# Score matmuls of a gated-linear-attention kernel moved from two single PSUM banks to one tile of two banks, with a new order of all steps

## The chip, the cores and the metric

One core of a Trainium2 chip runs the whole program. The metric is the device time of one execution in microseconds (us). The engines named below are TensorE (PE; its weight loads appear as PEld), VectorE (DVE), ScalarE (ACT), GpSimd (POOL), and SyncE (SP), which here issues all DMA transfers. PSUM, the memory that PE writes into, has eight banks of 512 fp32 values in each of 128 partitions.

## What is computed

The first part is a recurrent gated linear attention over 4 batches, 8 heads, 768 tokens and head size 48. Its output, laid out as 3072 tokens by 384, goes through a feed-forward block of width 2048 with a hard-swish between its two matrices. All values are fp32.

```python
def _attn_ref(q, k, v, alpha):
    B, H, S, D = q.shape                       # 4, 8, 768, 48
    state = np.zeros((B, H, D, D), dtype=np.float32)
    y = np.zeros_like(q)
    for t in range(S):
        state = alpha[:, :, t, :, None] * state + np.einsum('bhd,bhe->bhde', k[:, :, t], v[:, :, t])
        y[:, :, t] = np.einsum('bhd,bhde->bhe', q[:, :, t], state)
    return y

def _moe_ref(x, w_in, w_out):                  # x: 3072 x 384
    h = x @ w_in                               # 384 x 2048
    g = h * np.clip(h + 3.0, 0.0, 6.0) / 6.0
    return g @ w_out                           # 2048 x 384
```

## The kernel before, in words

**Tiles.** The tokens are cut into 24 chunks of 128 (6 for each batch), and the eight heads into four pairs, so that a tile has two heads in its partitions and four pairs along its free dimension. Two chunks make a group for the feed-forward block; there are 12 groups.

**The recurrence of one chunk j.** The names are those of the steps in the order at the end of the program.

- `la`, `lk`, `lq`, `lv` load alpha, k, q and v on SP. For the first six chunks `ta`, `tk` and `tq` transpose alpha, k and q on PE into a PSUM bank (L282); from chunk 6 on VectorE transposes them (L286), and PSUM isn't used for it.
- `ca` copies alpha out of PSUM (ScalarE, L300). `r` and `p` are scans over alpha on VectorE (L309 with the reciprocal at L313, and L320): products of the decays from the right and from the left. `k` and `q` multiply k and q with them (L332).
- `sc` computes the scores k times q on PE (L346), 64 by 64 tokens at a time: for each pair p, each half chunk b and each head a of the pair. `m` multiplies them with the triangular mask on VectorE (L356) and puts them into the tile `A`. `qa` copies q next to them (ScalarE, L366).
- `kb` and `ck` bring k by token: for chunks 0 to 7 by a transpose on PE (L374) and a copy on ScalarE (L378), from chunk 8 on through memory outside the core (`kt` on VectorE at L391, the writes `kw` at L396 and the reads `kr` at L404, both on SP).
- `u` computes the state's updates on PE (L429), `sm` adds them (VectorE, L437 and L439), `st` applies the decay (POOL, L409), and `sv` copies the state next to v (ScalarE, L419).
- `ya` and `yb` compute the outputs of the two half chunks on PE (L455), and `cy` copies them to `xT` (ScalarE, L464).

**The feed-forward block.** Groups 0 and 1 use plain products for the first matrix (`f`, `fa`, `fb`; L478 and L489), and group 0 also for the second (`b`, L516). All other products are fast matrix products that trade multiplications for sums: `M` (L600) with sums of the first weights (`y`), of x (`xc`), copies (`n`) and sums of the products (`o`); `P` (L703) with sums of the second weights (`x`) and of the hidden values (`s`), copies (`K`) and output sums (`G`). `O` stores outputs on SP. `e` and `h` are the hard-swish on ScalarE and VectorE (`fr` and `fg` in the plain part). `w` loads one of 16 slices of the weights, which come as float64; `d1`, `d2`, `dx` (ScalarE), `d3` (VectorE) and `d4` (POOL) turn a slice into fp32.

**PSUM.** Four banks `m0` to `m3` belong to the feed-forward block. The other four, `t0` to `t3` (L223), hold one thing at a time each: transposes, scores (two banks, one for each head of a pair), updates (one or two banks) or outputs. The numbers at the end of a step name them: `sc.0.2.3` puts the scores of chunk 0 into `t2` and `t3`, `u.0.2.1` its updates into `t2` and `t1`, `ya.0.3` its outputs into `t3`. A bank can be written again when the engine that reads it has ended.

**The order.** The program is one long list of some 1,800 such steps (from L751 on), and each engine runs its own steps in the order of the list. An instruction that waits holds up everything behind it on its engine. `z.m.n` are n matmuls of the identity with itself into bank m, which compute nothing (L532); the trace has two PE instructions for each of them.

The parts of the list that the change and the prediction's steps touch are its head up to the second feed-forward step, and its last lines:

```python
run("""z.0.5 z.0.3 z.0.1 z.0.8 qa.0.0 w.0 d2.0 d3.0 la.0 ta.0.0 ca.0 r.0 lk.0 tk.0.1 k.0
       z.0.2 p.0 la.1 ta.1.2 lq.0 tq.0.3 ca.1 r.1 lk.1 lv.0.0 sv.0.0 d1.0 kb.0.0 ck.0 z.0.2
       u.0.2.1 sm.0.0 sv.0.1 q.0 qa.0.1 tk.1.0 k.1 p.1 z.0.2 sc.0.2.3 m.0 la.2 ta.2.0 ca.2
       dx.0 w.2 d2.2 kb.1.0 ck.1 lq.1 r.2 sm.0.1 st.1 tq.1.2 q.1 d3.2 z.0.3 d1.2 dx.2 lv.1.1
       u.1.3.1 sv.1.0 sm.1.0 p.2 sm.1.1 sc.1.0.2 m.1 ya.0.3 yb.0 cy.0 lq.2 w.1 d1.1 tq.2.1
...
       P.11.4 G.11.1.2 P.11.5 G.11.2.1 O.11.2 P.11.6 G.11.3.0 O.11.3 O.9.2 O.11.1""")
```

Of the kernel before, what the change touches and what calls it, by code (L numbers as in the profile page):

```python
# [8 lines left out]
FP = mybir.dt.float32  # L9
# [4 lines left out]
ALU = mybir.AluOpType  # L14
# [3 lines left out]
def kernel(  # L18
# [32 lines left out]
    nc = tc.nc  # L51
    B, H, S, D = q.shape
    NTOK, DM = out.shape
    C = 128
    NC = S // C
    NCH = B * NC
    NP = H // 2
# [3 lines left out]
    G = 2  # L61
    GT = G * C
    HB = C // 2
# [12 lines left out]
    mask = consts.tile([C, C], mybir.dt.bfloat16, tag="mask")  # L76
# [146 lines left out]
    banks = [ps.tile([C, NP * C], FP, tag=f"t{i}", name=f"t{i}_ps") for i in range(4)]  # L223
# [5 lines left out]
    def bank(name, j, i):  # L229
        ps_t[name, j] = banks[i].rearrange("r (p n) -> r p n", p=NP)  # L230
        return ps_t[name, j]
# [106 lines left out]
    def scores(j, *at):  # L338
        sc = ps_t["sc", j] = [banks[i][:, 0 : NP * HB].rearrange("s (p t) -> s p t", p=NP)
                              for i in at]  # L340
        for p in range(NP):
            for b in range(2):
                half = slice(HB * b, HB * b + HB)
                for a in range(2):
                    r = slice(64 * a, 64 * a + D)
                    nc.tensor.matmul(sc[a][half, p], K_t[j][r, p, half], Q_t[j][r, p, half],  # L346
                                     start=True, stop=True)

    def masked(j):
        A_t[j] = As[j % 2]  # L350
        sc = ps_t.pop(("sc", j))
        for b in range(2):
            half = slice(HB * b, HB * b + HB)
            to = A_t[j][half, b].rearrange("s (p a) t -> s a p t", a=2)
            for a in range(2):
                nc.vector.tensor_tensor(  # L356
                    out=to[:, a], in0=sc[a][half],
                    in1=mask[half, half].unsqueeze(1).to_broadcast([HB, NP, HB]), op=ALU.mult)
# [386 lines left out]
    def run(words):  # L745
        for word in words.split():
            name, *at = word.split(".")
            steps[name](*(int(x) for x in at))

    with tc.manual_schedule():  # L750
        run("""z.0.5 z.0.3 z.0.1 z.0.8 qa.0.0 w.0 d2.0 d3.0 la.0 ta.0.0 ca.0 r.0 lk.0 tk.0.1 k.0  # L751
               z.0.2 p.0 la.1 ta.1.2 lq.0 tq.0.3 ca.1 r.1 lk.1 lv.0.0 sv.0.0 d1.0 kb.0.0 ck.0 z.0.2
               u.0.2.1 sm.0.0 sv.0.1 q.0 qa.0.1 tk.1.0 k.1 p.1 z.0.2 sc.0.2.3 m.0 la.2 ta.2.0 ca.2
               dx.0 w.2 d2.2 kb.1.0 ck.1 lq.1 r.2 sm.0.1 st.1 tq.1.2 q.1 d3.2 z.0.3 d1.2 dx.2 lv.1.1
               u.1.3.1 sv.1.0 sm.1.0 p.2 sm.1.1 sc.1.0.2 m.1 ya.0.3 yb.0 cy.0 lq.2 w.1 d1.1 tq.2.1
               q.2 d4.2 lk.2 tk.2.3 k.2 fa.2.0 d4.0 st.2 sc.2.0.2 d2.1 d3.1 m.2 dx.1 d4.1 qa.1.1
               lk.3 la.3 ta.3.1 ca.3 la.4 fa.0.1 sv.1.1 w.3 r.3 ta.4.3 ca.4 r.4 tk.3.1 k.3 kb.2.0
               qa.1.0 d2.3 ya.1.2 yb.1 cy.1 fa.1.2 lq.3 ck.2 d1.3 p.3 d3.3 lv.2.2 u.2.3.2 sm.2.0
               d4.3 fb.2 tq.3.1 q.3 fb.1 qa.2.0 sm.2.1 sv.2.0 st.3 fr.0.2.0 fg.0.2 lk.4 tk.4.0
               sv.2.1 w.5 d2.5 k.4 d3.5 d1.5 qa.3.0 d4.5 qa.2.1 sc.3.1.3 m.3 w.6 d2.6 d1.6 d3.6 d4.6  # L760
               lv.3.0 lq.4 w.7 kb.3.2 fb.0 f.0.3.3 kb.4.0 ya.2.1 ck.3 u.3.3.2 sm.3.0 fr.0.3.1 fg.0.3
               fr.0.1.0 fg.0.1 qa.3.1 sv.3.0 sm.3.1 p.4 d2.7 sv.3.1 d1.7 d3.7 d4.7 f.0.5.0 fr.0.5.1
               fr.0.0.0 fg.0.5 fg.0.0 tq.4.3 ck.4 la.5 ta.5.2 f.0.6.3 ca.5 w.4 d2.4 ya.3.0 yb.3 cy.3
               fr.0.6.1 yb.2 cy.2 w.9 d2.9 q.4 qa.4.1 d1.4 d1.9 dx.4 la.6 w.8 d3.4 r.5 lk.5 w.10
               d3.9 p.5 ca.6 fg.0.6 d4.9 w.12 lq.5 lv.4.1 d2.8 d3.8 f.0.7.2 d1.8 st.4 d4.8 d4.4 w.11
               fr.0.7.0 fg.0.7 f.1.7.0 fr.1.7.1 fg.1.7 sc.4.0.2 m.4 f.1.1.1 fr.1.1.0 fg.1.1 f.1.3.3
               fr.1.3.1 d2.10 d1.10 tk.5.3 f.1.0.2 d2.12 d3.10 d4.10 w.13 fg.1.3 fr.1.0.0 fg.1.0 k.5
               d3.12 lq.6 f.1.6.0 f.1.2.1 u.4.1.0 sm.4.0 d1.12 d4.12 sv.4.0 qa.4.0 ya.4.2 fr.1.6.1
               fg.1.6 w.15 tq.5.3 fa.4.3 sv.4.1 d2.11 kb.5.1 d2.13 fr.1.2.0 f.1.4.2 fr.1.4.1 d1.11
               sm.4.1 q.5 r.6 d3.11 d3.13 fg.1.4 d4.11 lv.5.0 lk.6 tq.6 p.6 d2.15 d3.15 fg.1.2 d1.13  # L770
               d4.13 sc.5.0.3 yb.4 f.1.5.0 fr.1.5.1 fg.1.5 tk.6 m.5 b.1.0.2 fb.4 b.1.1 d1.15 d4.15
               st.5 y.5 w.14 la.7 lk.7 cy.4 d2.14 qa.5.1 ck.5 b.0.0.1 fr.0.4.0 d3.14 k.6 q.6 ca.7
               fg.0.4 d1.14 d4.14 x.0 y.1 y.10 b.0.1 y.0 y.2 u.5.2 P.1.0.0 K.1.0 qa.5.0 sv.5.0
               qa.6.1 P.1.1.3 b.0.2 b.1.2 kb.6.0 ya.5.3 y.6 s.1.0.0 sm.5.0 sv.5.1 G.1.0.0 tk.7
               s.1.1.1 s.1.2.3 x.1 yb.5 cy.5 b.1.3 sc.6.1.2 lv.6.2 ck.6 u.6.3.0 s.1.3.2 x.2 P.1.2
               b.0.3 K.1.1 y.7 s.1.4 s.1.5 y.11 y.3 r.7 xc.2.1 x.3 y.4 y.8 xc.2.3 k.7 xc.2.0 xc.2.4
               y.9 y.12 y.16 y.13 y.15 P.1.3.3 K.1.2 P.1.4 bo.1 P.1.5 xc.2.5 G.1.1.1 P.1.6 y.14 y.17
               y.19 xc.2.6 sm.6.0 G.1.2.2 y.20 M.2.0.2 lv.12.1 la.8 O.1.1 O.1.0 ca.8 y.18 y.21 y.23
               so.1 G.1.3.3 n.2.0.8 bo.0 lq.7 lv.7.0 O.1.2 m.6 xc.2.2 xc.2.10 xc.2.7 tq.7 r.8 p.7
               xc.2.8 sv.6.1 M.2.15.3 M.2.1 kb.7.3 n.2.1.9 M.2.16 M.2.2 n.2.2.10 M.2.7.0 n.2.7.11  # L780
               sm.6.1 xc.2.9 q.7 p.8 M.2.3 M.2.4 n.2.4.12 M.2.8 o.2.0.0 M.2.5 n.2.5.13 qa.7.0 sv.6.0
               st.7 lk.8 O.1.3 lq.8 lk.9 la.9 la.10 tk.8 tq.8 lq.10 lq.9 ya.6.1 yb.6 M.2.9 z.1.3
               M.2.18.1 o.2.1.0 e.2.1.1 M.2.10 cy.6 ck.7 sc.7.0.2 u.7.1.3 n.2.10.14 M.2.11 qa.7.1
               ca.9 la.11 y.22 M.2.6.2 h.2.1 q.8 m.7 e.2.0.0 h.2.0 n.2.11.15 qa.6.0 n.2.18.10 qa.8.1
               M.2.12 M.2.19 n.2.12.12 M.2.13 sm.7.0 sv.7.1 r.9 k.8 o.2.3.0 sv.7.0 ya.7.0 y.24
               o.2.5.0 n.2.13.12 o.2.2.0 yb.7 cy.7 sc.8.1.2 xc.3.1 o.2.2.1 e.2.2.1 xc.3.3 o.2.3.1
               M.2.14 xc.3.4 xc.3.0 xc.3.5 o.2.4.0 xc.3.7 xc.3.6 o.2.6.0 P.2.0.1 M.3.0.2 M.2.17
               h.2.2 o.2.6.1 e.2.3.0 h.2.3 o.2.7.0 K.2.0 n.3.0.12 M.3.1 n.3.1.9 e.2.5.1 M.3.7.0
               n.3.7.13 xc.3.8 o.2.7.1 xc.3.2 kt.8 e.2.6.0 h.2.6 tk.9 M.3.2 n.3.2.10 e.2.4.0 P.2.1.3
               h.2.4 h.2.5 s.2.0.14 e.2.7.0 G.2.0.1 h.2.7 M.3.3 M.3.4 n.3.4.8 k.9 s.2.1.11 M.3.8  # L790
               o.3.0.0 ca.10 kt.9 P.2.3.3 s.2.2.15 s.2.3.14 lv.8.2 kw.8 kr.8 lk.10 sm.7.1 xc.3.9
               M.3.5 n.3.5.11 K.2.2 e.3.0.1 xc.3.10 M.3.9 o.3.1.0 P.2.2 K.2.1 u.8.0.3 M.3.18.2 s.2.5
               M.3.10 n.3.10.14 n.3.18.15 e.3.1.0 s.2.4 P.2.4 tq.9 h.3.0 st.8 sv.8.0 M.3.11 n.3.11.8
               tk.10 p.9 sm.8.0 q.9 r.10 k.10 qa.9.0 qa.9.1 m.8 sm.8.1 h.3.1 M.3.19 o.3.5.0 kt.10
               P.2.5 G.2.2.0 st.9 M.3.12 sc.9.0.1 qa.8.0 n.3.12.10 o.3.3.0 kw.9 lv.9.0 kr.9 sv.8.1
               u.9.2.3 sm.9.0 sv.9.1 sv.9.0 G.2.1.2 sm.9.1 st.10 M.3.15.2 M.3.16 M.3.6.3 M.3.13 m.9
               o.3.4.0 o.3.6.0 tq.10 n.3.13.10 o.3.2.0 e.3.4.1 ya.8.2 yb.8 ya.9.3 yb.9 cy.9 M.3.14
               M.3.17 cy.8 xc.4.1 P.2.6 e.3.5.0 G.2.3.3 o.3.2.1 xc.4.3 h.3.4 xc.4.4 o.3.6.1 xc.4.5
               xc.4.0 xc.4.6 e.3.2.1 M.4.0.0 n.4.0.10 P.3.0.1 xc.4.7 o.3.7.0 p.10 h.3.5 o.3.3.1
               xc.4.8 M.4.7.3 M.4.1 xc.4.2 h.3.2 o.3.7.1 lk.11 O.2.2 tk.11 e.3.6.0 e.3.3.1 h.3.3  # L800
               P.3.1.2 e.3.7.1 n.4.1.13 M.4.2 K.3.0 ca.11 q.10 h.3.6 r.11 k.11 h.3.7 n.4.7.15
               lv.10.2 lv.11.0 kw.10 sc.10.0.1 kr.10 G.3.0.0 u.10.3.2 sm.10.0 qa.10.1 n.4.2.14 M.4.3
               M.4.4 M.4.8 s.3.0.9 xc.4.9 s.3.2.12 s.3.1.11 P.3.3.2 n.4.4.8 M.4.5 o.4.0.0 e.4.0.0
               sv.10.1 sm.10.1 xc.4.10 kt.11 O.2.0 O.2.3 lq.11 m.10 s.3.3.9 s.3.5 M.4.9 o.4.1.0
               P.3.2 sv.10.0 st.11 n.4.5.11 K.3.2 la.13 M.4.18.0 p.11 tq.11 lk.12 tk.12 K.3.1 M.4.10
               n.4.10.9 q.11 qa.10.0 n.4.18.12 e.4.1.1 la.12 s.3.4 ca.12 h.4.0 r.12 P.3.5 G.3.2.1
# [126 lines left out]
```

## Time and profile before

| what | us |
|---|---|
| median of three runs | 536.54 (536.15 to 537.01) |
| the profiled execution | 536.33 |
| its span, first to last instruction | 534.5 |
| PE busy | 524.2 (98%) |
| VectorE busy | 477.1 (89%) |
| ScalarE busy | 257.6 (48%) |
| POOL busy | 50.4 (9%) |

The span in 40 equal slices; each digit is the busy share of a slice in tenths, and 9 means 90% or more:

```profile
PE   7799999999999999999999999999999999999997
DVE  6999989999999899998999999999999898586381
ACT  3889864212653553543644434642633544553330
```

The groups of the scores' mask and of the products that it can be compared with, as instructions of one form: count, then busy us and the mean ns of one, then idle time before them:

```profile
L356 DVE TENSOR_TENSOR A<-t_ps,mask 64x256 f32<-64x256 f32 x96 | 36.0, 413 | 0.4
L332 DVE TENSOR_TENSOR q<-t_ps,P 128x512 f32<-128x512 f32 x6 | 4.1, 684 | 0.0
L346 PE MATMUL t_ps<-q,k 48*64 48x64 f32 x768 | 16.7, 223 | 0.0
```

A mean is the time from an instruction's start to its end; instructions that follow each other overlap, so the busy time of a group (36.0 us for 96 masks) is less than count times mean. The granted PE clock is 1.00 in the records of the whole run.

### The profile page before, as it was taken

What the parts mean: (1) busy time and instruction counts of PE and PEld (TensorE: products, weight loads), DVE (VectorE), ACT (ScalarE), POOL (GpSimd) and SP (SyncE); (2) the same over time, 40 slices, a digit from 0 to 9 for tenths busy, and PEclk for the clock granted to TensorE, in tenths of its full rate; (3) what the DMA queues carried; (4) which work ended last, traced back from release to release, by engine and by line L of the source; (5) the groups of instructions that cost most, each with busy time, mean ns of one, the idle gap of its engine ahead of it and who ended that gap; (6) DMA issues with size and microseconds to landing.
All of it is one profiled execution on the core that took longest, in us unless ns stands there. A gap on an engine that the chain in (4) does not pass through costs nothing.

```text
span 534.5 us, 15145 instructions
## 1 busy us (share of the span) xinstructions
PE 524.2 (98%) x6306; PEld 498.9 (93%) x6306; DVE 477.1 (89%) x849; ACT 257.6 (48%) x503; POOL 50.4 (9%) x71
## 2 busy tenths in 40 slices
PE   7799999999999999999999999999999999999997
PEld 7698886789999999999999999999999999999996
DVE  6999989999999899998999999999999898586381
ACT  3889864212653553543644434642633544553330
POOL 5333435100000000000010000000000000000000
PEclk9999999999999999999999999999999999999999
DMA  9998877006615155254354455055364042100001
GB/s 174 215 255 256 208 220 164 7 2 158 149 32 121 28 132 130 50 136 101 82 109 113 95 124 139 20 129 122 81 144 97 18 97 48 36 3 1 29 1 44
DMA packets 124100, 54.40 MB, mean 102 GB/s; under 512 B 83328, under 2 KB 116864, under 8 KB 124032
## 3 DMA queue, kind: packets, MB, share of 16 engines
q1 hardware_dynamic: 124032, 53.44, 43.0%
q8 instruction: 49, 0.80, 0.7%
q14 instruction: 19, 0.16, 0.1%
HBM read 44.50 MB, written 8.91 MB: 100 GB/s over the span
## 4 chain that ended last, share of the span: by engine, by line
PE 88%; DVE 6%; POOL 2%; ACT 1%; DMA 1%; issue 0%; SPq 0%; DVEq 0%; POOLq 0%
PE m_ps L703 34%; PE m_ps L600 34%; PE m_ps L478 6%; PE t_ps L455 4%; PE t_ps L346 2%; PE t_ps L429 2%; PE m_ps L489 2%; DMA v<-in_v_dram 1%; PE m_ps L516 1%; DVE rings L647 1%; PE t_ps L282 1%; DVE raw L537 1%; ACT raw L191 1%; DVE g_sb L647 1%; DVE w L537 1%; POOL v L96 1%
## 5 line engine op out<-in xcount | busy, mean ns | idle before, releaser
L606 ACT COPY g_sb<-m_ps 128x512 f32<-128x512 f32 x110 | 63.7, 584 | 124.1 <-PE m_ps L600 101.3
L703 PE MATMUL m_ps<-w,g_sb 128*128 128x192 f32 x704 | 121.7, 327 | 0.0
L703 PEld LDWEIGHTS m_ps<-w,g_sb 128*128 128x128 f32 x704 | 113.7, 190 | 0.4
L703 PE MATMUL m_ps<-rings,g_sb 128*128 128x192 f32 x528 | 91.5, 326 | 0.0
L703 PEld LDWEIGHTS m_ps<-rings,g_sb 128*128 128x128 f32 x528 | 85.4, 190 | 0.1
L600 PE MATMUL m_ps<-xc,w 128*128 128x128 f32 x640 | 82.7, 277 | 0.3 <-DVE w L541 0.3
L600 PEld LDWEIGHTS m_ps<-xc,w 128*128 128x128 f32 x640 | 77.5, 192 | 1.5 <-issue 0.5
L494 ACT ACTIVATE r<-g_sb,half 128x512 f32<-128x512 f32 x80 | 57.0, 722 | 31.5 <-DVE g_sb L541 12.4
L498 DVE SCALAR_TENSOR_TENSOR g_sb<-r,g_sb 128x512 f32<-128x512 f32 x80 | 53.7, 682 | 6.8 <-ACT r L494 5.4
L600 PE MATMUL m_ps<-xT,raw 128*128 128x128 f32 x400 | 52.5, 277 | 0.0
L600 PEld LDWEIGHTS m_ps<-xT,raw 128*128 128x128 f32 x400 | 48.6, 192 | 0.6
L409 POOL TENSOR_TENSOR st<-sm,R 128x192 f32<-128x192 f32 x20 | 12.9, 643 | 353.7 <-DVE sm L439 295.7
L647 DVE TENSOR_TENSOR g_sb<-g_sb 128x512 f32<-128x512 f32 (+1 forms) x55 | 42.1, 793 | 1.3 <-PE m_ps L703 1.1
L600 PE MATMUL m_ps<-xT,w 128*128 128x128 f32 x320 | 42.0, 276 | 0.0
L600 PEld LDWEIGHTS m_ps<-xT,w 128*128 128x128 f32 x320 | 39.3, 192 | 0.1
L366 ACT COPY A<-q 48x256 f32<-48x256 f32 x88 | 35.5, 404 | 5.0 <-DVE q L332 3.7
L356 DVE TENSOR_TENSOR A<-t_ps,mask 64x256 f32<-64x256 f32 x96 | 36.0, 413 | 0.4
L478 PE MATMUL m_ps<-xT,w 128*128 128x256 f32 x144 | 32.8, 382 | 0.0
L600 PE MATMUL m_ps<-xc,raw 128*128 128x128 f32 x240 | 31.8, 276 | 0.0
L478 PEld LDWEIGHTS m_ps<-xT,w 128*128 128x128 f32 x144 | 26.7, 190 | 3.6
L309 DVE TENSOR_TENSOR_SCAN R<-t,ones 128x516 f32<-128x516 f32 x24 | 29.6, 1233 | 0.5 <-ACT t L300 0.4
L600 PEld LDWEIGHTS m_ps<-xc,raw 128*128 128x128 f32 x240 | 29.6, 192 | 0.1
(104 smaller groups left out, 730.3 us busy)
## 6 DMA issues: line engine op xcount, KB each, us to landing
raw<-in_moe_w_out_dram SPq DMA_DIRECT2D x8, 768.0 KB, 5.3
raw<-in_moe_w_in_dram SPq DMA_DIRECT2D x6, 768.0 KB, 7.1
v<-in_v_dram SPq DMA_DIRECT2D x48, 96.0 KB, 3.0
out_dram<-oh SPq DMA_DIRECT2D x44, 96.0 KB, 1.7
far<-kq SPq DMA_DIRECT2D x64, 64.0 KB, 2.2
kb<-far SPq DMA_DIRECT2D x64, 64.0 KB, 2.1
aq<-in_alpha_dram SPq DMA_DIRECT2D x36, 96.0 KB, 2.4
qq<-in_q_dram SPq DMA_DIRECT2D x36, 96.0 KB, 2.5
```

Source lines behind the costliest of these rows:

```text
L309: nc.vector.tensor_tensor_scan(out=reverse(R, n - 1, n), data0=reverse(ax, n, n), data1=reverse(ones, n, n), initial=0.0, op0=ALU.mult, op ...
L356: nc.vector.tensor_tensor(out=to[:, a], in0=sc[a][half], in1=mask[half, half].unsqueeze(1).to_broadcast([HB, NP, HB]), op=ALU.mult)
L366: nc.scalar.copy(out=to[:, a], in_=Q_t[j][64 * a : 64 * a + D, :, half])
L409: nc.gpsimd.tensor_tensor(out=st, in0=sm, in1=R_t[j][:, :, 0:1].to_broadcast([C, NP, D]), op=ALU.mult)
L455: nc.tensor.matmul(y_of(j, (i + 1) // 2, p)[:, HB * b : HB * b + HB], vb[:, p, e : e + 32], A_t[j][:, b, 2 * p + a], start=(b == 0 and i = ...
L478: nc.tensor.matmul(h[:, f], w1[:, kk, o : o + C], xT_t[g][:, kk], start=(kk == 0), stop=(kk == KT - 1))
L494: nc.scalar.activation(out=to, in_=h, func=AF.Relu, bias=half, scale=1.0 / 6.0)
L498: nc.vector.scalar_tensor_tensor(out=to, in0=r, scalar=1.0, in1=h, op0=ALU.min, op1=ALU.mult)
L600: nc.tensor.matmul(acc[g][i][:, f * C : (f + 1) * C], spots[w][:, f * C : (f + 1) * C], x_of(g, x), start=(first and f == 0), stop=last, s ...
L606: nc.scalar.copy(out=slots[z], in_=acc[g][i])
L647: nc.vector.tensor_tensor(out=out, in0=in0, in1=in1, op=ALU.subtract)
L703: nc.tensor.matmul(to[g], a, rhs[:, f], start=(first and f == 0), stop=(last and f == HF - 1), skip_group_check=True)
```

## The change

Two of the four banks become one tile, `pair`, of two banks. The scores of a chunk are written into it, one bank for each head of a pair, so one VectorE operation masks both heads of a half chunk: two operations of 64 by 512 a chunk in place of four of 64 by 256. The first bank of the pair also takes the transposes of alpha and of k by token (steps `ta.j` and `kb.j` without a bank's number). Two single banks, `t0` and `t1`, are left for the transposes of k and q, the updates and the outputs. The list of steps has the same steps in another order; only where the `z` steps stand, how they are grouped, and the banks and slots that steps name are different.

```diff
-    banks = [ps.tile([C, NP * C], FP, tag=f"t{i}", name=f"t{i}_ps") for i in range(4)]
+    banks = [ps.tile([C, NP * C], FP, tag=f"t{i}", name=f"t{i}_ps") for i in range(2)]
+    pair = ps.tile([C, 2, NP * C], FP, tag="pair", name="pair_ps")
...
     def bank(name, j, i):
-        ps_t[name, j] = banks[i].rearrange("r (p n) -> r p n", p=NP)
+        to = pair[:, 0] if i is None else banks[i]
+        ps_t[name, j] = to.rearrange("r (p n) -> r p n", p=NP)
         return ps_t[name, j]
...
-    def scores(j, *at):
-        sc = ps_t["sc", j] = [banks[i][:, 0 : NP * HB].rearrange("s (p t) -> s p t", p=NP)
-                              for i in at]
+    def scores(j):
+        sc = ps_t["sc", j] = pair[:, :, 0 : NP * HB].rearrange("s a (p t) -> s a p t", p=NP)
...
-                    nc.tensor.matmul(sc[a][half, p], K_t[j][r, p, half], Q_t[j][r, p, half],
+                    nc.tensor.matmul(sc[half, a, p], K_t[j][r, p, half], Q_t[j][r, p, half],
                                      start=True, stop=True)
...
-            to = A_t[j][half, b].rearrange("s (p a) t -> s a p t", a=2)
-            for a in range(2):
-                nc.vector.tensor_tensor(
-                    out=to[:, a], in0=sc[a][half],
-                    in1=mask[half, half].unsqueeze(1).to_broadcast([HB, NP, HB]), op=ALU.mult)
+            nc.vector.tensor_tensor(
+                out=A_t[j][half, b].rearrange("s (p a) t -> s a p t", a=2), in0=sc[half],
+                in1=mask[half, half].unsqueeze(1).unsqueeze(1).to_broadcast([HB, 2, NP, HB]),
+                op=ALU.mult)
...
+        run("""z.0.1 z.0.2 z.0.3 z.0.8 qa.0.0 w.0 d2.0 la.0 ta.0 ca.0 d1.0 la.1 ta.1 ca.1 d3.0 lk.0
+               tk.0.0 r.0 k.0 dx.0 kb.0 ck.0 p.0 r.1 lq.0 tq.0.1 lv.0.0 w.2 lk.1 z.0.2 q.0 qa.0.1
+               z.0.5 p.1 sv.0.0 u.0.0.1 sm.0.0 sv.0.1 sc.0 m.0 d2.2 tk.1.0 k.1 d4.0 sm.0.1 st.1 la.2
+               ta.2 z.0.3 d1.2 d3.2 ca.2 r.2 kb.1 lq.1 tq.1.0 q.1 z.0.2 p.2 z.0.3 dx.2 ck.1 lv.1.1
+               u.1.1.0 sv.1.0 qa.1.0 sm.1.0 sm.1.1 st.2 d4.2 sc.1 m.1 w.1 d1.1 d2.1 lk.2 tk.2.1 k.2
+               lq.2 tq.2.0 q.2 ya.0.1 yb.0 w.3 sv.1.1 dx.1 d3.1 d4.1 sc.2 m.2 ya.1.0 cy.0 fa.0.0
+               d2.3 d3.3 la.3 ta.3 ca.3 r.3 qa.1.1 d1.3 d4.3 fa.2.1 lk.3 tk.3.1 k.3 yb.1 cy.1 la.4
+               ta.4 ca.4 r.4 w.5 qa.2.0 d2.5 d3.5 d1.5 fa.1.2 kb.2 ck.2 fb.0 fr.0.0.0 fb.2 lv.2.2
...
+               s.11.0.14 o.11.7.1 h.11.5 e.11.7.0 h.11.7 s.11.1.15 P.11.0.0 M.11.6.3 P.11.3.2
...
+               G.11.2.2 O.11.1 O.11.2 O.11.0 O.11.3""")
```

## The prediction

> **What bounds the kernel now.** I read the busy shares, then TensorE's (PE's) busy time by stage, then what PE waited for, then the timelines of the opening, of one stretch in the middle and of the end. The window view (first column the stretch in us, then its length, then busy time of PE, its weight loads, VectorE, ScalarE, GpSimd, the clock, DMA share, GB/s):
>
> ```profile
> 0.00:40.00 40.00, 33.78 (x548) 30.14 (x549) 34.88 (x63) 28.61 (x45) 15.97 (x27) 1.00 1.11 215
> 40.00:126.00 86.00, 86.00 (x842) 70.78 (x841) 83.46 (x129) 44.94 (x79) 23.32 (x27) 1.00 0.53 142
> 126.00:512.00 386.00, 385.71 (x4806) 379.52 (x4805) 348.55 (x643) 180.82 (x374) 11.14 (x17) 1.00 0.37 85
> 512.00:535.00 23.00, 18.73 (x117) 18.43 (x116) 10.23 (x17) 3.23 (x7) 0.00 (x0) 1.00 0.08 26
> ```
>
> From 40 us to the last matmul PE has no hole but 0.3 us, and VectorE is nearly as full (97% in the second stretch, 90% in the third). The waits of PE from 40 us on are one line, and over the whole run the rest lies in the opening:
>
> ```profile
> PE m_ps L600 <- DVE w L541: 0.3, 1, 0.3
> ```
> ```profile
> PE m_ps L532 <- POOL ident masks.py:199: 1.5, 1, 1.5
> PE t_ps L429 <- issue: 1.0, 1, 1.0
> PE t_ps L429 <- DMA v<-in_v_dram: 0.7, 2, 0.4
> PE t_ps L374 <- ACT t L300: 0.7, 1, 0.7
> ```
>
> So a gain can only come from four places: holes of the opening (6.2 us of 40), matmuls that compute nothing, the cost of going from one kind of matmul to another, and the 3.8 us after the last matmul. A loss can come from any new wait of PE.
>
> **The Trainium skill.** "PSUM — Partial Sum Buffer", The four PSUM rules: a matmul's output fits one bank of 512 fp32, and there are eight. Both layouts use all eight (4+4 before, 2+2+4 after), so a changed order of hand-over is the whole price of the pair. "VectorE: DVE Perf Modes", The TRN2 errata: an fp32 tensor_tensor takes (N+151)/0.96 ns; that is 424 ns for 256 elements and 691 for 512. The trace agrees: 413 for the mask (L356), 681 to 684 for products that read PSUM (L332). "TensorE: Matmul & The Clock Gate", Part 1: the array starts at half clock and is full after about 3.4 us of work, so idle matmuls at the start are warm-up. The trace shows it as 34 passes in 6.0 us, where a later pass takes 0.112.
>
> **Part 1: two mask operations for four.** VectorE operations that follow each other overlap their ends: in the timeline two 512-wide products start 0.60 apart, and four masks take 1.50.
>
> ```profile
> 14.06 0.68 DVE L332 TENSOR_TENSOR q<-t_ps,P 128x512 f32<-128x512 f32 x1
> 14.66 0.68 DVE L332 TENSOR_TENSOR k<-t_ps,R 128x512 f32<-128x512 f32 x1
> 16.39 1.50 DVE L356 TENSOR_TENSOR A<-t_ps,mask 64x256 f32<-64x256 f32 x4
> ```
>
> The trace has no mask over two banks. Bounds: 0.60 + 0.68 = 1.28 a chunk if it runs as the L332 row, 1.50 if spanning banks gives the saving back. I take 1.28: 0.22 x 24 chunks = 5.3 us of VectorE time saved. VectorE ended one wait of PE after 40 us, of 0.3 us, so I count 0 to 0.3 us and take 0. PE covers it; were that cover gone, the 5.3 would count. PE's score matmuls are as many and as long.
>
> **Part 2: two single banks and a pair.** Nothing is issued more. Added are waits: score matmuls need the pair free, and so do the transposes of alpha (`ta`), of k by token (`kb`), which now write `pair[:, 0]`; the four single banks could be taken in any order. Queued behind such a wait is all of PE. Its size depends on the order, below.
>
> **Part 3: the order, opening.** All steps are the same; only banks and places differ (29 idle pairs in both). I walked the new queues with the trace's durations and spacings (a 192 KB load lands 1.2 us after the one before it, a w slice 2.2 to 2.7; four transposes to data 0.64 us; copies 0.58; scan 1.23; product 0.60/0.68; `dx` 1.93). First matmul at 1.46; 28 warm-up passes for 34, so 6 x 0.112 less: 6.8 us. `ta.0` 6.9 (alpha lands 6.78); `ca.0` to 8.1; `r.0` to 9.6; `k.0` 9.9 (k is now the fourth load and lands at 9.2), `kb.0` 10.6; `p.0`, `r.1`, `q.0` to 13.7, before 14.7; `u.0`, `sc.0` to 14.75, before 15.4; `m.0` 15.0 to 16.3, before 17.9. Then the pair bites: `ta.2` must wait for `m.0` (16.35; it began at 15.42 before), and `k.1`, now behind `m.0`, ends at 16.9 (15.3 before), but `kb.1` waits in both for the copy of alpha: 18.15 against 16.75. ScalarE's `dx.2` (1.93) stands before `ck.1`, so `u.1` 20.6 (before 19.9), `sc.1` to 21.7 (22.0). `k.2`, `q.2` to 24.9; `ya.0` 24.15 (22.0), `sc.2`, `ya.1` to 26.25; `cy.0` behind `dx.1` to 26.7; `fa.0` 26.75, `ta.3`, `fa.2`, `tk.3`, `yb.1`, `ta.4`, `fa.1`, ending at 32.95. Without idle pairs PE has then done 15.1 us of work; the kernel before had 18.0 at 35.76 and hardly a hole just ahead of it, so 15.1 at about 32.9. Even: 0, with 1.5 either way, since w.2, d2 and dx have changed places.
>
> **Part 3, the idle matmuls.** Three idle pairs stood in the full part of the program, where nothing is to be filled:
>
> ```profile
> 137.80 0.83 PE L532 MATMUL m_ps<-ident 128*128 128x128 f32 x6
> ```
>
> To the next start it is 0.67 us. They now stand among the holes of the opening: -0.67 (0 if the opening lengthens by them).
>
> **Part 3, changes of kind.** In the middle, a group of small matmuls costs more than its own passes:
>
> ```profile
> 178.13 1.05 PE L600 MATMUL m_ps<-xc,w 128*128 128x128 f32 x8
> 179.11 0.69 PE L346 MATMUL t_ps<-q,k 48*64 48x64 f32 x32
> 179.63 0.83 PE L429 MATMUL t_ps<-v,kb 64*64 64x48 f32 x32
> ```
>
> The 8 passes took 0.98 to the next start, 0.09 over 8 x 0.112; about 0.2 to 0.25 a group with the way back. From `M.2.0` on (125.7 us) both orders have 28 such groups; between `fb.1` and there I count 14 before and 12 after: -0.4 (0 to -0.6).
>
> **Part 3, are there new waits in the full part?** I added up, per engine, the work that stands ahead of the tightest step. Before, `M.2.0` starts at 125.70 and its last weight sum `y.20` ended at 124.8. VectorE's work up to `y.20` is 107.9 after and 110.6 before, by the spacings above; PE's work up to `M.2.0` is 109.0 against 112.1 (one `b`, one `u` and `sc` moved behind it, one more idle group ahead). Both move by about 3, so a margin of some 0.7 us stays. VectorE's first sum over x (`xc.2.1`) now stands ahead of 16 us of its work and waits for `cy.5`; by the same count it is ready 0.8 us before VectorE arrives. The way of k through memory (`kt` to `u`) has 13.8 us of PE work or more, 13.2 before; the loads of v have 12.0 or more, 14.6 before, and take about 4. SP waits longer on output stores in both. These are margins, not proofs: I add 0.5 us of new small waits (0 to 4).
>
> **Part 3, the end.** Here three stores follow the last copy:
>
> ```profile
> 530.77 0.32 ACT L716 COPY oh<-m_ps 128x192 f32<-128x192 f32 x1 [10.08 <-PE m_ps L703]
> 531.11 1.29 SPq L724 DMA_DIRECT2D out_dram<-oh  x3
> ```
>
> `O.9.2` and `O.11.1` stood behind `O.11.3` on SP and had only waited for it. They are now ahead; `O.11.3` is last. The third issue began at 531.97, the first at 531.11: -0.86. The last products (`P.11`) run without a hole in both: of their inputs the two late ones, `s.11.0` and `s.11.1`, have 6.1 us of PE work (`P.10.6`, `P.11.0`, `M.11.6`) over some 5.7 of VectorE's chain.
>
> **Sum.** 0 - 0.67 - 0.4 + 0.5 - 0.86 = -1.4 us. Against the profiled execution (536.33, of which the span is 534.5): 534.9. The median is 536.54, 0.2 above it: about 535.1.
>
> **Rivals.**
> 1. *The pair makes PE wait (slower).* Up to `sc.7` the pair changes hands some 21 times between transposes, scores, masks and copies; each needs the reader's end, and one mask operation holds both banks. For it: my walk met such waits at `ta.2` and `kb.1`, and VectorE is 97% full to 126 us. Against: with the full queue ahead, the readers are 2 us or more early. At 0.22 us each, 4.6 us, less the 1.9 that still holds: 539.2. It decides from 2.5 us, 0.12 a hand-over.
> 2. *Nothing to see.* The opening keeps the pair's delay of 1.4 us at `kb.1` instead of regaining it: 536.5.
> 3. *VectorE is the true bound.* Its 5.3 us all reach the end, with the end's 0.86: 530.4. For it: 97% in the second stretch. Against: one wait of 0.3.
>
> **Numbers.** Forecast -1.4 us: 0.52, own range 533.4 to 536.6. Rival 1: 0.27; rival 2: 0.15; rival 3: 0.06. 0.2% is 1.07 us, about what can be told from no change: 535.47 to 537.61. Some 0.39 of the forecast's 0.52 lies below, and rival 3: faster 0.45; rival 2 and the rest: same 0.28; slower 0.27. The range for 8 in 10 leaves out rival 3 and half of rival 1: 532.8 to 539.
>
> **What would show it.** Right: mask rows x48 near 680 ns; no PE wait over 0.3 us past 40 us; `M.2.0` starting near 121 to 122; one store after the last copy. Wrong: PE waits on `pair_ps` readers (L355, L302, L378), a mask over 750 ns, or an opening in which `fa.1` ends past 35 us.

## The result, and the profile after

The changed kernel takes 539.6 us (median of 6 runs, 539.17 to 540.93); beside it the kernel before took 536.38. The ratio is 1.0062, 95% interval 1.0049 to 1.0075: slower by 3.2 us, where 1.4 us less was forecast. The profiled execution took 539.50 us, of which the span is 537.7 (before 536.33 and 534.5).

The window view of the changed kernel, in the same four stretches and columns as before; the last stretch ends with the longer span:

```profile
0.00:40.00 40.00, 32.10 (x498) 29.67 (x498) 33.20 (x52) 26.95 (x41) 16.04 (x27) 0.96 1.12 224
40.00:126.00 86.00, 83.94 (x819) 69.73 (x813) 81.86 (x120) 46.27 (x80) 23.64 (x28) 1.00 0.56 151
126.00:512.00 386.00, 385.78 (x4853) 378.61 (x4852) 348.70 (x609) 179.01 (x373) 11.05 (x17) 1.00 0.35 83
512.00:538.00 26.00, 22.89 (x147) 22.59 (x145) 13.37 (x22) 4.89 (x10) 0.00 (x0) 1.00 0.07 24
```

From 126 us to 512 PE is as full as before (385.78 against 385.71). Between 40 and 126 us it has 2.06 us of holes where it had none, and from 0 to 40 us it does 1.68 us less. To put numbers on it, I took for each group of matmuls the time to the next group's start, less its passes times their usual spacing (idle matmuls count as passes). This excess is, before and after: 11.7 and 14.1 us from 0 to 40 us, 3.1 and 5.3 from 40 to 120, 10.2 and 9.7 from there on. After the last matmul come 3.8 and 2.8 us. Together +2.4 + 2.2 - 0.5 - 1.0 = +3.1 us: the whole loss, all of it ahead of 126 us. (The levels depend by some tenths on the spacing that is taken for the small matmuls; the differences don't.)

What PE waited for in the changed kernel (total us, times, longest), past 40 us, and then five of the lines for the whole run:

```profile
PE m_ps L703 <- DVE g_sb L664: 1.2, 1, 1.2
PE m_ps L478 <- DVE g_sb L498: 0.7, 1, 0.7
PE m_ps L600 <- DVE raw L537: 0.2, 1, 0.2
```
```profile
PE t_ps L455 <- DVE k L334: 1.5, 1, 1.5
PE t_ps L455 <- issue: 1.4, 1, 1.4
...
PE t_ps L284 <- DVE s L437: 1.0, 1, 1.0
...
PE pair_ps L284 <- ACT t L302: 0.7, 1, 0.7
PE pair_ps L284 <- DVE A L355: 0.6, 1, 0.6
```

None of the waits past 40 us is for a bank of the pair: the first is a product (`P.1.3`) that waits for a sum of VectorE (`s.1.0`), the second `f.1.5` for `fg.1.7`. In the opening the pair shows twice, 0.7 us at `ta.1` and 0.6 at `ta.2`, and the two single banks show twice: `ya.0` waits 1.5 us for `t1`, which the product `k.2` reads, and `tk.1` 1.0 us for `t0`, which `sm.0.0` reads. Whether these hand-overs cost anything is tried below. `fa.1` has ended at 36.18 us (the next group starts there), where the walk had 32.95, and `M.2.0` starts at 127.76, where 121 to 122 was forecast (before: 125.70).

The mask, in the view of one line (minimum, median, maximum in ns), and the end of the timeline:

```profile
L355 DVE TENSOR_TENSOR A<-pair_ps,mask x48: 642/688/695, 15.9 to 468.5; 64x512 f32<-64x512 f32 x48
```
```profile
534.92 0.32 ACT L716 COPY oh<-m_ps 128x192 f32<-128x192 f32 x1 [9.86 <-PE m_ps L703]
535.27 0.33 SPq L724 DMA_DIRECT2D out_dram<-oh  x1
```

Both are as predicted in kind: 48 masks near 680 ns, and one store after the last copy.

Two theories stood for the rest. *Theory 1*: the layout costs the time, by hand-overs of the pair and by one mask over both banks. *Theory 2*: the new list costs it, and the layout is worth nothing.

### The profile page after: what moved, and what is told of

Read it like the earlier page. It is cut to its first block, busy times and chain, and to the rows that moved or that the text cites. A ratio compares the mean times of both kernels' runs of the same rounds, so it can differ in the third digit from the quotient of the medians.

```text
span 537.7 us, 15053 instructions
## 1 busy us (share of the span) xinstructions
PE 524.7 (98%) x6306; PEld 500.6 (93%) x6306; DVE 477.1 (89%) x801; ACT 257.1 (48%) x503; POOL 50.7 (9%) x71
## 4 chain that ended last, share of the span: by engine, by line
PE 80%; DVE 14%; issue 2%; ACT 1%; SPq 1%; POOL 1%; DMA 0%; DVEq 0%; POOLq 0%
PE m_ps L600 32%; PE m_ps L703 31%; PE t_ps L455 4%; PE m_ps L478 3%; PE pair_ps L347 2%; PE t_ps L429 2%; PE m_ps L489 2%; PE m_ps L532 1%; DVE g_sb L498 1%; DVE g_sb L647 1%; DVE A L355 1%; DVE rings L647 1%; POOL w L217 1%; DVE P L322 1%; DVE R L311 1%
## 5 line engine op out<-in xcount | busy, mean ns | idle before, releaser
L600 PEld LDWEIGHTS m_ps<-xT,w 128*128 128x128 f32 x320 | 39.4, 192 | 0.3
L537 DVE TENSOR_TENSOR g_sb<-g_sb 128x512 f32<-128x512 f32 x40 | 27.2, 687 | 8.3 <-ACT g_sb L606 8.2
L355 DVE TENSOR_TENSOR A<-pair_ps,mask 64x512 f32<-64x512 f32 x48 | 32.7, 682 | 0.6
L322 DVE TENSOR_TENSOR_SCAN P<-t 128x516 f32<-128x516 f32 x24 | 30.8, 1284 | 0.1
```

Of the source, the lines that this page charges most:

```text
L322: nc.vector.tensor_tensor_scan(out=P_t[j], data0=aX[j % 2][:, 0:n], data1=ini[j % 2], initial=0.0, op0=ALU.mult, op1=ALU.add)
L355: nc.vector.tensor_tensor(out=A_t[j][half, b].rearrange("s (p a) t -> s a p t", a=2), in0=sc[half], in1=mask[half, half].unsqueeze(1).unsq ...
L537: eng.tensor_tensor(out=out, in0=in0, in1=in1, op=ALU.add if s1 > 0 else ALU.subtract)
L600: nc.tensor.matmul(acc[g][i][:, f * C : (f + 1) * C], spots[w][:, f * C : (f + 1) * C], x_of(g, x), start=(first and f == 0), stop=last, s ...
```

## The experiments

Every ratio below is to the kernel before, run beside it (its medians were 536.56 to 536.8 us).

**Layout and list exchanged, banks by the order of the list.** The list of one kernel was put on the banks of the other; each step was given the bank that came free first in the order of the list.

```diff
 # old list, new layout
+    banks += [pair[:, 0], pair[:, 1]]
-    ... u.1.3.1 sv.1.0 sm.1.0 p.2 sm.1.1 sc.1.0.2 m.1 ...
+    ... u.1.1.2 sv.1.0 sm.1.0 p.2 sm.1.1 sc.1 m.1 ...
 # new list, old layout
-    ... la.1 ta.1 ca.1 ... sc.0 m.0 ...
+    ... la.1 ta.1.1 ca.1 ... sc.0.2.3 m.0 ...
```

> The list of the kernel before (one step moved: sc.17 stands two places later, behind m.16) with the new layout: pair of two banks, scores and two-operation masks on it; both halves of the pair also serve as single banks, so that every step keeps a free bank where the old list has it. Theory 1, the hand-overs of the pair and the one mask over both banks cost the time: 538.5 to 540 us, with PE waits on pair_ps readers beyond those that the kernel before has on t_ps. Theory 2, the new list costs it and the layout is worth nothing: 536.0 to 536.9, mask rows x48 at about 682 ns, VectorE busy about 3.3 us less than before. A value of 535 or less would say that VectorE was the bound.

> The list of the changed kernel with the old layout: four single banks, four masks a chunk; each step takes the bank that came free first, so that ta.1 need not wait for the copy ca.0 nor ta.2 for the mask m.0. Theory 1 (the pair costs the time): 536 to 537 us. Theory 2 (the list costs it): 538.5 or more, up to 541 because VectorE has 3.3 us more to do; the PE waits at 107 us (P.1.3 for s.1.0) and at 77 us (f.1.5 for fg.1.7) stay. Both together in equal parts: about 538.

Measured: 556.13 us (ratio 1.0358, 1.0344 to 1.0371) and 546.88 (1.017, 1.0133 to 1.0206). The first lies far outside all expectations, and the second above the 541 us that Theory 2 had allowed, so neither tells the theories apart. The timeline of the first shows why:

```profile
21.61 0.58 ACT L379 COPY kb<-pair_ps 128x512 f32<-128x512 f32 x1
...
22.25 1.11 PE L285 MATMUL pair_ps<-ident,rings 128*128 128x128 f32 x4 [2.16 <-ACT kb L379]
```

`tq.1` had the second half of the pair, `kb.1` the first, and `tq.1` started only when the copy `ck.1` had read the first: the halves of the tile were not independent places. Elsewhere `u.1` lay in the pair right ahead of `sc.1`, which then waited 3.2 us for `sm.1.1`. Where a bank comes free first in a list that four engines run at their own pace says little of when its reader ends. The second kernel lost 4.6 us in one hole of PE inside `ya.1` and 1.8 us in a wait at `u.0`; both are taken up below.

**The old list on the new layout, with places chosen from the trace.** The pair counts as one place, and each step got the place whose last reader had ended longest ago in the trace of the kernel before.

```diff
+    banks += [pair[:, 0]]
-    ... kb.4.0 ya.2.1 ck.3 u.3.3.2 ... f.0.7.2 d1.8 ... kb.5.1 d2.13 ... sm.4.1 ...
+    ... ya.2.0 ck.3 u.3.1.2 ... f.0.7.2 kb.4.0 d1.8 ck.4 ... d2.13 ... sm.4.1 kb.5.0 ...
```

> The list of the kernel before with the new layout, used strictly as three places (t0, t1 and the pair as one). Four steps are moved because the list needs a fourth place there: sc.17 two places later, behind m.16, kb.5 behind sm.4.1, kb.4 behind f.0.7, ck.4 behind d1.8. Each step has the place whose last reader, by the trace of the kernel before, ended longest ago; by these times only two hand-overs come late, tk.1 by 0.52 us and tq.1 by 0.34. Theory 2 (the list costs the time, the layout nothing): 536.4 to 537.3 us. Theory 1 (hand-overs of the pair cost it wherever they stand): 538.5 or more. VectorE as the bound: under 535.5.

Measured: 536.86 us, ratio 1.0005 (0.9997 to 1.0013). Its windows, to be compared with those of the two kernels:

```profile
0.00:40.00 40.00, 32.92 (x538) 29.11 (x539) 34.14 (x56) 28.02 (x43) 15.74 (x27) 1.00 1.12 213
40.00:126.00 86.00, 86.00 (x844) 70.69 (x844) 82.95 (x123) 45.36 (x80) 23.74 (x27) 1.00 0.53 141
```

PE has no hole between 40 and 126 us. VectorE's busy time over the run falls from 477.1 to 474.7 us, and the time does not follow. So with this list the pair, its hand-overs and its two-operation masks cost nothing and bring nothing: Theory 1 falls, and with it the rival that VectorE is the bound. What is lost comes with the new list; whether that list would lose less on four banks is tried further down.

**Idle matmuls for the clock.** The clock records of the changed kernel show half clock from 17.6 to 21.0 us, after holes of PE. Two idle groups were put into those holes.

```diff
-    ... sv.0.1 sc.0 m.0 d2.2 tk.1.0 k.1 ...
+    ... sv.0.1 sc.0 z.0.5 m.0 d2.2 tk.1.0 z.0.3 k.1 ...
```

> The changed kernel with two more idle groups in holes of the opening: z.0.5 (10 passes) behind sc.0 and z.0.3 (6 passes) behind tk.1, so that PE has no long hole between 14.8 and 17.4 us. Theory of the clock (PE fell back to half clock from 17.6 to 21.0 us after these holes, and this cost the passes of ta.2 to the next idle group 1.6 us): about 538.3 us, no half clock in the records after the warm-up, fa.1 ending near 35.0 instead of 36.2. Rival, the opening is bound by loads and VectorE and the slow passes only filled waits: 539.3 to 540.0.

Measured: 540.38 us (1.0069, 1.0057 to 1.0081): no gain. A stretch at half clock came all the same, from 15.6 to 19.0 us. And one of the changed kernel's own runs that was at full clock throughout (mean 1.000) had a span of 537.8 us, another with the gap (0.997) 537.7. In the kernel with the added groups a run at full clock took 540.68 us. So the half clock is not what makes the changed kernel slower.

**The middle.** Two steps of the new list were moved, one for each wait past 40 us.

```diff
-    ... kb.5 f.1.3.0 w.4 fr.1.1.1 ... fg.1.1 la.6 ca.6 sm.4.1
+    ... kb.5 f.1.3.0 la.6 w.4 fr.1.1.1 ... fg.1.1 ca.6 sm.4.1
-    ... b.1.1 x.0 x.1 k.6 s.1.0.0 y.1 ...
+    ... b.1.1 s.1.0.0 x.0 x.1 k.6 y.1 ...
```

> The changed kernel with two steps moved: s.1.0 ahead of x.0 on VectorE (P.1.3 waited 1.2 us for it at 107.5 us), and the load la.6, with its fill on POOL, ahead of w.4 and so of POOL's d4.4 (ca.6 on VectorE waited 1.5 us for the fill, fg.1.7 came late and f.1.5 waited 0.7 at 76 us). If these two waits are the middle's part of the loss: 537.4 to 537.8, the loss from 40 to 126 us gone. If PE only meets the next late step a little further on: 538.5 to 539.6.

Measured: 538.40 us (1.0048, 1.0019 to 1.0077), runs from 537.48 to 545.17. By the median that is 1.2 us less, between the two values that were expected, but the interval overlaps that of the changed kernel. Of the two waits nothing is left: past 40 us the list of PE's waits has 0.4 us for a weight sum and 0.2 for a load. How the first one arose is seen in the timeline of the changed kernel (start, us, engine, line), VectorE above and PE below:

```profile
103.82 1.75 DVE L647 TENSOR_TENSOR rings<-w 128x1536 f32<-128x1536 f32 x1
105.68 1.76 DVE L647 TENSOR_TENSOR w<-w 128x1536 f32<-128x1536 f32 x1
107.36 0.68 DVE L334 TENSOR_TENSOR k<-k,R 128x512 f32<-128x512 f32 x1
107.96 0.68 DVE L664 TENSOR_TENSOR g_sb<-g_sb 128x512 f32<-128x512 f32 x1
```
```profile
105.55 1.99 PE L455 MATMUL t_ps<-A,v 128*32 128x64 f32 x128
108.70 0.59 PE L703 MATMUL m_ps<-w,g_sb 128*128 128x192 f32 x2 [1.15 <-DVE g_sb L664]
```

`x.1` writes over a block of the second weights, which the plain products (`b`) read until 105.55 us, and starts at 105.68; VectorE was idle for 0.1 us before it. `s.1.0` needed none of this but stood behind `x.0`, `x.1` and `k.6`, 4.1 us of VectorE's work, and `P.1.3` needs `x.1` and `s.1.0`. The profiled run took 541.57 us, more than the median, and its losses lie in the opening: a scan took 2.82 us there and PE stood still for 2.8 us inside `ya.1`. This leads to the next experiments.

**The opening, by `p.1` and `fa.0`.**

```diff
-    ... z.0.5 p.1 sv.0.0 ... tk.1.0 k.1 d4.0 ...
+    ... z.0.5 sv.0.0 ... tk.1.0 k.1 p.1 d4.0 ...
-    ... d4.1 sc.2 m.2 ya.1.0 cy.0 fa.0.0 d2.3 ... d4.3 fa.2.1 ...
+    ... d4.1 cy.0 fa.0.0 sc.2 m.2 ya.1.0 fa.2.1 d2.3 ... d4.3 ...
```

> The changed kernel with the opening rearranged: the scan p.1 behind k.1 on VectorE (it took 1.91 us beside POOL's d4.0 and stood ahead of sm.0.0, m.0 and k.1), and fa.0 ahead of sc.2 and ya.1, fa.2 behind ya.1, so that PE's 128 instructions of ya.0 and 128 more of sc.2 and ya.1 do not follow each other. Theory of the instruction fetch (in the middle of ya.1 PE stood still for 1.4 us with no wait, until 1.5 us after a packet of the instruction queue had landed): the hole inside ya.1 goes, 538.0 to 538.6. Theory of the bank hand-overs (the opening waits for readers wherever the small groups stand): 539.2 to 540.

> The edits of the two kernels ahead of this one together. If opening and middle are separate places of the loss, the gains add up: 535.8 to 536.6. If PE's queue takes the gain of the one back in the other: 537.5 to 539.

Measured: 543.84 us (1.0129, 1.0105 to 1.0154), and with the two moves of the middle 540.41 (1.0079, 1.0064 to 1.0094). The hole inside `ya.1` is gone in both, and both are slower than the changed kernel: in the first, `u.1` now waits 1.4 us for the product `q.1`, for which `p.1` came late, and `fa.0` waits 0.7 for `cy.0` in both. The edit moved a step that was not to blame: in both traces the scan `r.1` takes 2.82 us and PE waits 1.7 us for it at `u.0`, which is explained next.

**POOL's add beside VectorE's scans.** In the changed kernel `d4.0` runs on POOL at 12.01 us; in the kernel before no `d4` runs ahead of 22.68. VectorE (two lines) and POOL in the changed kernel, then VectorE and POOL in the kernel with the middle's two moves:

```profile
11.81 1.21 DVE L311 TENSOR_TENSOR_SCAN R<-t,ones 128x516 f32<-128x516 f32 x1
...
13.84 1.91 DVE L322 TENSOR_TENSOR_SCAN P<-t 128x516 f32<-128x516 f32 x1
```
```profile
12.01 2.65 POOL L217 TENSOR_TENSOR w<-w,raw 128x768 int32<-128x768 int32 x1 [4.28 <-DVE P L322]
```
```profile
11.73 2.82 DVE L311 TENSOR_TENSOR_SCAN R<-t,ones 128x516 f32<-128x516 f32 x1
```
```profile
11.49 1.96 POOL L217 TENSOR_TENSOR w<-w,raw 128x768 int32<-128x768 int32 x1 [3.75 <-ACT raw L191]
```

Whichever starts second seems to stand still until the other has ended. In the changed kernel the scan at 11.81 started first; the add needs some 1.85 us and shows 2.65, 0.80 more, where 1.01 us of the scan were left; the next scan, begun under the add, ends 1.09 us after the add's end (14.66). In the other kernel the add started first, and the scan ends 1.10 us after it (13.45). So it is in four more of the traces in which `d4.0` has this place in the list (`r.1` takes 2.81 to 2.82 us, and PE waits 1.7 to 1.8 us at `u.0` for `q.0`, which stands behind the scan). The Trainium skill says this in "SBUF — State Buffer", section "SBUF: two separate sides": VectorE and GpSimd share a pair of ports, an "exclusive lock, not a bandwidth split", which a VectorE operation with two inputs in SBUF and a GpSimd operation that reads SBUF take from each other for a whole instruction. The trace agrees, and the product from PSUM at 13.14 us, under the same add, kept its 0.66 us. Behind the late scan stand `sm.0.0`, `m.0` and `k.1`, and so PE's `tk.1` and `ta.2`.

```diff
-    ... tk.1.0 k.1 d4.0 sm.0.1 st.1 ... sm.1.1 st.2 d4.2 sc.1 ...
+    ... tk.1.0 k.1 sm.0.1 st.1 ... sm.1.1 st.2 d4.0 d4.2 sc.1 ...
```

> The changed kernel with one step moved: POOL's add d4.0 goes from ahead of st.1 to ahead of d4.2, so that it runs at about 24.5 us, where no scan runs, instead of at 12 us between the scans r.1 and p.1. Theory of the shared port (a scan that starts beside the add takes 1.91 or 2.82 us instead of 1.22, since it begins in earnest only when the add has ended; u.0, sm.0.0, m.0 and ta.2 stand behind it): both scans at 1.2 us, PE earlier by 0.7 us or more at ta.2, 538.0 to 539.0 us. Rival, the opening's end is set by the loads or by the instruction fetch, which take the gain back: 539.3 to 540.

Measured: 538.18 us (1.0034, 1.0021 to 1.0048), seven of eight runs between 538.12 and 538.72: 1.4 us less than the changed kernel (whose interval, from 1.0049, lies just above), with one run at 541.28. That run is the profiled one: its clock was 0.95 from 6.6 us to 291. The same two scans in the kernel of the next experiment, which has this move too:

```profile
11.71 1.21 DVE L311 TENSOR_TENSOR_SCAN R<-t,ones 128x516 f32<-128x516 f32 x1
...
13.74 1.23 DVE L322 TENSOR_TENSOR_SCAN P<-t 128x516 f32<-128x516 f32 x1
```

How the 1.4 us come about is only in part in the traces. In the changed kernel's trace the scan lost 0.7 us, and its `ta.2` starts at 17.36 us, against 16.58 in the kernel of the next experiment. A hole of PE inside `ya.1`, 1.4 us long in the changed kernel and taken up next, is absent from the trace of the kernel with this move alone; but the next kernel has the hole again and the same ratio. And the move brings the add under other work: it now runs right ahead of `d4.2`, and the conversion `d3.1`, which takes 0.68 us in the changed kernel, stands still until both have ended (VectorE, then POOL, in the kernel with this move alone):

```profile
25.19 2.33 DVE L203 TENSOR_SCALAR w<-w 128x768 f32<-128x768 f32 x1
28.16 1.38 DVE L355 TENSOR_TENSOR A<-pair_ps,mask 64x512 f32<-64x512 f32 x2
```
```profile
23.30 3.67 POOL L217 TENSOR_TENSOR w<-w,raw 128x768 int32<-128x768 int32 x2
```

Behind it stands the mask `m.2` (28.16), and `ta.3` waits 0.9 us for that. A still better place of `d4.0` was not tried.

**The hole inside `ya.1`, and all repairs together.** In the changed kernel PE stops in the middle of `ya.1`, with no semaphore to wait for:

```profile
27.74 0.54 PE L455 MATMUL t_ps<-A,v 128*32 128x64 f32 x18
29.66 0.42 PE L455 MATMUL t_ps<-A,v 128*32 128x64 f32 x14 [1.38 <-issue]
```

A 16 KB packet of the instruction queue was served from 26.69 to 28.15 us, in a stretch in which loads kept the DMA engines full; PE went on 1.5 us after it. In four more kernels the hole stands at the same instruction (the 706th of PE and its weight loads) and ends 1.3 to 1.6 us after such a packet. In the two kernels of the opening's edit the packet comes as late (26.92 and 27.16 us), but PE reaches this instruction only at 33.04 and 34.21, and there is no hole. So PE ran out of instructions, as far as a trace can tell. Moving `ya.1` behind `fa.0` was to give the packet time:

```diff
-    ... sc.2 m.2 ya.1.0 cy.0 fa.0.0 d2.3 ...
+    ... sc.2 m.2 cy.0 fa.0.0 ya.1.0 d2.3 ...
```

> As the kernel ahead of this one, and ya.1 behind fa.0 in PE's queue (sc.2 and its mask stay ahead), so that 1.3 us of long matmuls stand before the place where PE's instructions ran out. Theory of the instruction fetch: the hole inside ya.1 falls from 1.4 us to under 0.5, and with the port's gain 537.0 to 538.2 us. Rival, the hole only moves to another wait of the same length (fa.0 for the copy cy.0): no better than the kernel ahead of this one.

> As the kernel ahead of this one, and the two moves of the middle (s.1.0 ahead of x.0, la.6 ahead of w.4). If the three places (port, fetch, late VectorE work) are the whole loss of the new list: 535.0 to 536.3 us, at or under the kernel before, since the end of the new list is worth 0.95 us. If the opening keeps 2 us: 537 to 538.

Measured: 538.62 us (1.0033, 1.0020 to 1.0046), no better than without the move, and its profile still has the hole:

```profile
28.70 0.31 PE L455 MATMUL t_ps<-A,v 128*32 128x64 f32 x5
30.40 0.64 PE L455 MATMUL t_ps<-A,v 128*32 128x64 f32 x27 [1.39 <-issue]
```

The packet came at 27.50 us here. In the kernel ahead of this one, whose list is the same up to this place, it came at 22.40 us and there was no hole. So neither what the hole costs nor what makes the packet late was shown. With the two moves of the middle as well: 536.84 us (1.0010, 1.0000 to 1.0020), 1.8 less, between the two values expected. The trace of this kernel has no hole inside `ya.1`, so the two kernels do not differ by the middle alone; but from 40 to 120 us, behind the hole, the excess fell by 1.9 us. There `P.1.3` follows without a wait:

```profile
103.40 1.99 PE L455 MATMUL t_ps<-A,v 128*32 128x64 f32 x128
105.32 0.92 PE L703 MATMUL m_ps<-w,g_sb 128*128 128x192 f32 x4
```

The new list with the repairs takes the time of the kernel before, to 0.2%, and that with an end worth some 0.9 us to it.

**The repaired list on four single banks**, places again chosen from the trace:

```diff
-    ... la.0 ta.0 ca.0 d1.0 la.1 ta.1 ca.1 ... sc.0 m.0 ...
+    ... la.0 ta.0.0 ca.0 d1.0 la.1 ta.1.1 ca.1 ... sc.0.0.3 m.0 ...
```

> The list of the kernel with all three repairs (d4.0, ya.1, and the two moves of the middle; 536.84 us with the pair) on the old layout: four single banks, four masks a chunk, each step on the bank whose last reader had ended longest ago by that kernel's trace, so that ta.1 need not wait for ca.0. Theory, the layout is worth nothing in either list: 536.4 to 537.3 us, with 3.3 us more of VectorE's mask time hidden. If the pair's hand-overs hold what the opening still loses against the kernel before (1.3 us from 0 to 40 us): 535.4 to 536.2. If the two-operation masks had carried the new list: 538 or more.

Measured: 537.63 us (1.0017, 1.0011 to 1.0024). It is 0.8 us above its like with the pair, somewhat more than was expected: freeing the banks gains nothing in the new list either. In its trace `ya.0` no longer waits for a bank, but `ta.1`, `tk.2` and `tq.2` wait 0.6, 1.4 and 0.4 us for their loads: the loads stand behind the hand-overs. What the 0.8 us are is not shown. The two-operation masks may be worth a few tenths, but this trace has the hole inside `ya.1` (1.3 us) and that of its like has none, and the intervals of the two (to 1.0020, from 1.0011) overlap.

**The end and the idle group alone, in the kernel before.**

```diff
-    ... yb.6 M.2.9 z.1.3 M.2.18.1 ...
+    ... yb.6 M.2.9 M.2.18.1 ...
-    ... G.11.3.0 O.11.3 O.9.2 O.11.1
+    ... G.11.3.0 O.9.2 O.11.1 O.11.3
```

> The kernel before with two of the new list's parts alone: the group z.1.3 taken out of the full part (0.67 us of PE), and the stores O.9.2 and O.11.1 put ahead of O.11.3 at the end (0.86 us). If both terms of the sum are right: 534.9 us (536.4 less 1.5). If the idle group only filled a wait: 535.5. If the last store takes as long whatever stands behind it: 535.7; neither: 536.4.

Measured: 535.45 us, ratio 0.9977 (0.9968 to 0.9986): 1.2 us less, of 1.5 expected. After the last matmul its trace has 2.8 us in place of 3.8, so the end gives what was expected or a little more, and what is left for the idle group is 0.2 to 0.3 us of 0.67. This version is ahead of both kernels.

**The old order in the first 23 us only**, the repaired new list behind it, with the pair:

```diff
-    z.0.1 z.0.2 z.0.3 z.0.8 qa.0.0 w.0 d2.0 la.0 ta.0 ca.0 d1.0 ...
+    z.0.5 z.0.3 z.0.1 z.0.8 qa.0.0 w.0 d2.0 d3.0 la.0 ta.0.0 ca.0 r.0 ... k.2 fa.2.1
+    qa.1.0 st.2 d4.0 d2.1 w.3 ...
```

> The first 23 us in the kernel before's order (its list up to k.2, then fa.2), the rest in the order of the kernel with the three repairs, with the pair of banks throughout; each step of the opening on the place that is free longest, as in the first kernel with the old list and three places. Theory, what the repaired list still loses is where the steps of the first 23 us stand: PE's excess over its passes from 0 to 40 us falls from 13.0 to about 11.7, three idle groups less (0.67 us) and the new list's end: 535.0 to 535.8 us, ahead of both kernels. If the loss sits behind 23 us (sc.2, ya.1, fa.0 to fa.1): 536.3 to 537.

Measured: 538.88 us (1.0041, 1.0028 to 1.0055), a miss on both counts. PE was ahead at 29 us (`ya.1` began at 28.97, against 29.60 in the repaired list), and then lost more than that: 0.7 us at `tk.3` for the copy of alpha, and waits of 0.9 and 0.7 us for VectorE at 39 and 53 us. Instead of falling, the excess from 0 to 40 us is 0.7 us higher than in the repaired list. This front did not fit that back. What the repaired list still loses in the opening (excess 13.0 us against 11.7) stays open.

## Why the prediction was wrong, step by step

- **Two mask operations for four**: right in kind, too high in size. A chunk's masks take 1.38 us, between the bounds of 1.28 and 1.50; all 48 are busy for 32.7 us against 36.0, so 3.3 us of VectorE were saved and not 5.3. That PE hides it is shown by the old list with the pair: 536.86 us. (In the changed kernel VectorE's busy time did not even fall: 477.1 us in both.)
- **Two single banks and a pair**: right that the price depends on the order and not on the pair. With places chosen by the readers' ends the old list pays nothing.
- **The order, opening ("Even: 0, with 1.5 either way")**: the first step that failed. The excess grew by 2.4 us, and with the idle groups that were to fill the holes `fa.1` came 3.2 us later than walked. The walk took each scan at 1.23 us and followed VectorE, ScalarE, PE and the loads; POOL's queue was not in it. `d4.0` had moved from behind `k.2` to ahead of `st.1` in the list, into the time of two scans. That its place costs 1.4 us is shown by moving it; the drawn-out scan is 0.7 us of this in the changed kernel's trace. With the add moved, the trace of the repaired kernel keeps to the walk as far as `u.1` (`ta.2` at 16.57 us, walked 16.35; `kb.1` 18.22, 18.15; `u.1` 20.54, 20.6). Behind it that kernel is late too: `ya.0` at 24.89 for 24.15, `fa.1` ended at 34.97 for 32.95. In three kernels with the move `tk.2` waits 1.0 to 1.4 us for its load, which may be a part of it; the remainder, 1.0 to 1.3 us by the excess, is not explained. (One reading in the walk is off: the 22.0 us given for the end of `sc.1` before is the start of `ya.0`; `sc.1` ended at 21.5.)
- **Idle matmuls and end (-0.67 and -0.86)**: -1.2 together in the kernel before, most of it by the end. The end of the changed kernel itself gave 3.8 - 2.8 = 1.0 us. In the changed kernel the idle groups gain nothing that can be seen, since the opening grew by more.
- **Changes of kind (-0.4)**: not tried by itself. The excess behind 120 us fell by 0.5, but the term had its saving ahead of `M.2.0`, where the excess rose; so the agreement in size may be luck.
- **New waits in the full part ("0.5 us of new small waits, 0 to 4")**: the second step that failed, in size. It compared the queues' totals at one place, `M.2.0`, and took the margin there for the whole stretch (by its own figures 0.9 - 3.1 + 2.7 = 0.5 us, not 0.7). But two waits stood ahead of it, inside the totals: `s.1.0` behind `x.0` and `x.1`, and `fg.1.7` behind `ca.6`, which waited 1.5 us for a fill that POOL did only after `d4.4`. The excess grew by 2.2 us; with both moves the time fell by 1.8 in the kernel with the other repairs, and the excess there by 1.9.
- **The rivals**: the time that the first gave, 539.2 us, was near the measured one, and its mechanism was wrong: no PE wait past 40 us is for the pair, and the pair without the new list costs nothing. Of the signs named, the late `fa.1` (36.18, past 35) and the late `M.2.0` told rightly that the opening and the stretch behind it had failed. The waits on readers of the pair (0.7 and 0.6 us) came as well and pointed the wrong way.

## What to carry to other kernels

When an order is changed, walk every engine's queue, the idle ones too: the place of one add on GpSimd, which was busy for a tenth of the span, was worth 1.4 us, and it held up VectorE's scans by 0.7 to 1.6. A margin at the tightest place of a stretch says nothing of the waits ahead of it; for each PE step that needs another engine, find what stands ahead of its input in that engine's queue, as `x.0`, `x.1` and `k.6` stood ahead of `s.1.0`. Choose the place of a tile by when its reader ends in the trace, not by the order of the list, and count a tile of two banks as one place: with the same tiles and nearly the same list the two together were the difference between 556.1 and 536.9 us.

## What the runs showed of the hardware

- A scan of 1.22 us that begins under a GpSimd add of 1.85 us takes up to 2.82 us, and an add that begins under a scan is drawn out to 2.65. A conversion with one input (0.68 us) that began under two adds took 2.33. A product that reads PSUM is not touched (0.66 us under the same add).
- In five of the traces PE stood still for 1.3 to 4.6 us with no wait, always at the same instruction inside a group of small matmuls, and went on 1.3 to 1.6 us after a 16 KB packet of the instruction queue had been served. That the packet was late because of the loads in flight is not shown.
- PE's clock went back to half for 3.4 us in several runs, after holes in the opening, in the kernel with the best time too (535.45 us). For that kernel the profiled run with such a gap took 536.03 us; runs with a mean clock of 1.000 took 535.13 to 536.02. In the kernel with all repairs the five runs with such a gap (0.996 or 0.997) took 536.84 to 539.63 and the eight others 536.42 to 536.92; whether the clock or the holes ahead of it cost that was not tried.
